# adaLN block with sliding-window attention and a token-mixing MLP: opening loads put on two DMA queues, and the last output tile cut at column 384 with a PSUM bank for each piece

## The chip, the cores and the metric

The kernel runs on one core of one Trainium2 chip. The metric is the device time of one execution in microseconds (us); smaller is better. The kernel before takes 256.79 us, the median of three runs (254.97, 256.79 and 257.36). The profile that is read here is one further execution, of 257.96 us; the span that it shows, from the core's first instruction to its last, is 256.3 us, and 1.66 us of the time lie around it.

## The reference

Everything is bf16 at the boundary. `x` has 2048 tokens of 512 columns. A condition vector `c` makes six modulation vectors, the block normalizes, attends in a window of 256 tokens with 32 heads of 16 columns, normalizes again and mixes over the tokens with an MLP of width 1792:

```python
mod = (silu(c) @ w_mod).reshape(1, 6, 1, 512)          # sa, ca, ga, sb, cb, gb
h = layernorm(x) * (1 + ca) + sa
q, k, v = split(h @ wqkv)                              # 32 heads of 16
p = softmax(where(0 <= i - j < 256, q @ k.T / 4, -1e9))
x = x + ga * ((p @ v) @ wo)
h = layernorm(layernorm(x) * (1 + cb) + sb)
u = gelu(einsum('bsd,sf->bdf', h, w1) + b1)            # over the tokens
x = x + gb * (einsum('bdf,fs->bds', u, w2) + b2).T
```

## The kernel before, in words

**Tiles.** Tokens are cut into 16 tiles of 128 (`NT`), columns into 4 slices of 128 (`ND`). `xres[t]` holds tile t of `x` in SBUF all the way through. Four groups of 512 tokens go through projection, attention (75 chunks: scores on TensorE, `et = exp` on ScalarE, a mask on VectorE, sums on TensorE), output projection and the second and third normalization. Then comes the MLP: `u` over tokens, gelu, and `y` back to tokens.

**Order.** Most of the kernel is recorded as operations with an engine each and issued in one order written out by hand (`ORDER`, run by `run_schedule`). `Ordered` wraps the engines so that the program keeps this order: on every engine, instructions run in the order in which they stand, and a waiting one holds what is behind it. Inside a helper all of these instructions carry line 256, so the profile is read by tile names. Two stretches stand outside the list: the opening loads (lines 343 to 376), issued before anything else, and the last loop (lines 1381 to 1398).

**The opening.** All loads but one go out on SyncE's DMA queue (SP): `x0`, `x1`, then the first 1024 columns of `w_mod` in four pieces of 256 KB (`wmod`, slice j = 0 to 3), then `wqkv` in pieces, then the rest. Only the 1 KB load of `c` (tile `c4`) goes out on ScalarE's queue (ACT), line 346. Each DMA has a completion semaphore; there are eight, taken in turn, so the ninth DMA issued waits, on the engine that issues it, until the first has landed, and so on.

What depends on these loads, in the order in which the engines have it:

- ScalarE: table load, (issue of `c`), `em`, `em`, `rm` (the sigmoid of `c` by exp, log, exp), the two `rs` of the first normalization, one half of the copy of the transposed tiles to `h1T`, one slice of the modulation of `h1T`.
- VectorE: statistics (`st`, `mv`) of `x0`, then `silu` (needs `rm`), then statistics of `x1`, the copy `sT`, the two normalized tiles `xn`, the other half of the copy to `h1T`, `modFM` (needs all four `wmod` slices), three slices of the modulation of `h1T`.
- TensorE: eight warm-up matmuls on a zero tile, the transpose of `silu` (`st_ps`), two more warm-ups, `fm` for slices 0 and 1 of `wmod` (tile `ps_fm`), eight transposes of `xn`, `fm` for slices 2 and 3, four warm-ups, then the first key and query projections (tiles `pss`, `pk`, `pq`), which need `h1T` and the first pieces of `wqkv`; then the first scores.

**The last loop.** For each of 16 token tiles, 14 matmuls of 512 columns add into one PSUM bank `py`; VectorE adds `xr` (a `scalar_tensor_tensor` made beforehand) and writes `otile`; SP sends it out. Banks are taken from the list `homes` in turn. The last tile is done in two halves of 256 columns, 14 matmuls each, both in the same bank, each half with its own add and its own DMA.

Of the kernel before, what the change touches and what calls it, by code (L numbers as in the profile page):

```python
# [13 lines left out]
P = 128  # L14
S = 2048
D = 512
# [3 lines left out]
NT = S // P  # L20
# [195 lines left out]
def kernel(  # L216
# [14 lines left out]
    nc = tc.nc  # L231
# [11 lines left out]
    F32 = DT.float32  # L243
# [19 lines left out]
    dma = Ordered(nc.sync)  # L263
# [63 lines left out]
    ps_od = ctx.enter_context(tc.tile_pool(name="ps_od", bufs=1, space=PSUM))  # L327
# [13 lines left out]
    c4 = modw.tile([ND, P], BF, name="c4")  # L341

    def load_x(t, queue=dma):
        queue.dma_start(out=xres[t][:], in_=x_dram[t * P : (t + 1) * P, :])

    nc.scalar.dma_start(out=c4[:], in_=c.rearrange("o (j p) -> (o j) p", p=P))

    def load_mod(j, queue):
        queue.dma_start(out=wmod[:, j, 0 : 2 * D], in_=wm_v[:, j, 0 : 2 * D])

    def load_qkv(lo, hi):
        dma.dma_start(out=wqkv[:, :, lo:hi], in_=w_v[:, :, lo:hi])

    load_x(0)
    load_x(1)
    for j in range(ND):
        load_mod(j, dma)
    load_qkv(D, D + D // 2)
    load_qkv(0, D // 2)
    load_qkv(D + D // 2, 2 * D)  # L360
# [112 lines left out]
    box = {}  # L473
# [16 lines left out]
    def e_stps(e):  # L490
# [13 lines left out]
        out=sT_rep[:], in_=sT[:].unsqueeze(2).to_broadcast([P, ND, P])), deps=[o6], pos=-6, ready=15.0)  # L504
# [64 lines left out]
    for g in range(ND):  # L569
        mod_ops.append(op("wod", "DVE", 0.34, lambda e, g=g: ve.tensor_tensor(  # L570
            out=wod[:, g, :], in0=wod[:, g, :], in1=bc_ga[:], op=ALU.mult), deps=[mod_ops[0]], pos=14.0, ready=30.0))
# [809 lines left out]
    w2r, gtmp = box["w2r"], box["gtmp"]  # L1381
    homes = ["t3", "t4", "od0", "od1", "od2", "t0", "t1", "t2"]
    for tb in range(NT):
        h = homes[tb % 8]
        py = (ps_od.tile([P, D], F32, name="py", tag=h) if h[0] == "o" else box["ps_t"].tile([P, D], F32, name="py", tag="ps" + h))
        xr = gtmp.tile([P, D], F32, name="xr")
        ve.scalar_tensor_tensor(
            out=xr[:], in0=bc_gb[:], scalar=b2FM[:, tb : tb + 1], in1=xres[tb][:], op0=ALU.mult, op1=ALU.add,
        )
        ot = gtmp.tile([P, D], BF, name="otile")  # L1390
        for cols in (slice(0, D),) if tb < NT - 1 else (slice(0, D // 2), slice(D // 2, D)):
            for n, fc in enumerate(order):
                te.matmul(
                    py[:, cols], lhsT=w2r[tb // 8][:, fc, tb % 8 * P : (tb % 8 + 1) * P], rhs=guT[fc][:, cols],
                    start=(n == 0), stop=(n == NF - 1), skip_group_check=True,
                )
            ve.tensor_tensor(out=ot[:, cols], in0=py[:, cols], in1=xr[:, cols], op=ALU.add)
            dma.dma_start(out=out_dram[tb * P : (tb + 1) * P, cols], in_=ot[:, cols])
# [31 lines left out]
```

## Time and profile before

| what | value |
|---|---|
| median of three runs | 256.79 us |
| profiled execution | 257.96 us, of which the span is 256.3 us |
| TensorE busy | 237.3 us (93% of the span) |
| VectorE busy | 209.5 us (82%) |
| ScalarE busy | 179.3 us (70%) |
| GpSimd busy | 127.6 us (50%) |
| mean granted TensorE clock | 0.993 |
| DMA | 28.12 MB, 110 GB/s over the span |
| chain that ended last | PE 52%, ACT 24%, DVE 15%, issue 5%, DMA 2%, SP's queue 1% |

The engines are PE (TensorE matmul), PEld (TensorE weight load, which overlaps PE), DVE (VectorE), ACT (ScalarE), POOL (GpSimd) and SP (SyncE); a q behind a name is the engine's own sequencer, which waits and issues DMAs. Busy shares are means over stages: in attention ScalarE runs without a break (39.79 of the 40 us from 20 to 60), in the MLP TensorE does. The chain of waits is followed back from the last instruction, at each step to what released it; its shares say which engine was being waited for. Matmuls are pipelined, so 14 matmuls of 0.38 us that start every 0.22 us are normal.

### The profile page before, as it was taken

The page shows a single profiled execution, that of the slowest core. Times are in us where ns is not written, and L with a number is a line of the kernel's source. Part 1 is how long each engine was busy: PE and PEld are TensorE (multiplying, and loading weights), DVE is VectorE, ACT ScalarE, POOL GpSimd, SP SyncE. Part 2 cuts the span into 40 slices and gives each one's busy share as a digit, 9 for nine tenths or more (in the row PEclk, how much of TensorE's full clock was granted, in tenths as well). Part 3 has the DMA queues.
Part 4 walks back from the last instruction along what each step waited for, and adds up shares of the span by engine and source line. Part 5 has one row for each costly group of instructions (what it writes and reads, how often), then busy time and mean ns, then how long its engine had stood idle before and what let it go on. Part 6 is the DMA issues. An engine that isn't in the chain of part 4 may idle for free.

```text
span 256.3 us, 9271 instructions
## 1 busy us (share of the span) xinstructions
PE 237.3 (93%) x3995; PEld 127.0 (50%) x3995; DVE 209.5 (82%) x412; ACT 179.3 (70%) x253; POOL 127.6 (50%) x225
## 2 busy tenths in 40 slices
PE   7798889899998779999999999899999999999994
PEld 3466545454554534554545455466444444444443
DVE  5579999999999999998898989999978964444442
ACT  4399999999999899999999999988136610000000
POOL 8267967799779467769773479762000000000000
PEclk9799999999999999999999999999999999999999
DMA  6998660133054200010403375322999101111111
GB/s 204 325 351 266 52 201 10 44 73 97 3 95 97 54 13 0 6 43 18 132 3 102 102 196 166 84 84 78 331 387 387 51 23 49 54 41 43 41 41 41
DMA packets 42624, 28.12 MB, mean 110 GB/s; under 512 B 12248, under 2 KB 38488, under 8 KB 42584
## 3 DMA queue, kind: packets, MB, share of 16 engines
q1 hardware_dynamic: 42576, 27.54, 36.9%
q8 instruction: 31, 0.51, 0.9%
q14 instruction: 9, 0.07, 0.1%
q10 hardware_dynamic: 8, 0.00, 0.0%
HBM read 22.03 MB, written 2.10 MB: 94 GB/s over the span
## 4 chain that ended last, share of the span: by engine, by line
PE 52%; ACT 24%; DVE 15%; issue 5%; DMA 2%; SPq 1%; DVEq 0%
ACT et L256 21%; PE py L256 19%; PE pu L256 14%; PE pss L256 6%; DVE et L256 6%; PE po L256 5%; PE pa L256 3%; ACT lz L256 2%; DVE h L256 2%; PE pk L256 2%; PE pq L256 2%; DMA wmod<-in_w_mod_dram 2%; DVE OT L256 1%; PE pv L256 1%; DVE QT L256 1%
## 5 line engine op out<-in xcount | busy, mean ns | idle before, releaser
L256 ACT ACTIVATE et<-pss 128x1536 bf16<-128x1536 f32 x75 | 110.6, 1474 | 3.6 <-PE psb L256 2.0
L256 DVE TENSOR_TENSOR et<-et,maskt 128x1024 bf16<-128x1024 bf16 (+2 forms) x79 | 49.0, 647 | 0.7 <-ACT et L256 0.7
L256 PE MATMUL py<-guT,w2r 128*128 128x512 bf16 (+1 forms) x238 | 48.7, 366 | 0.5 <-DVE otile L256 0.5
L256 ACT ACTIVATE et<-psb 128x512 bf16<-128x512 f32 x75 | 46.7, 622 | 0.0
L256 PE MATMUL pu<-hb,w1s 128*32 128x512 bf16 (+1 forms) x332 | 39.2, 380 | 0.4 <-DVE part L256 0.2
L256 PE MATMUL pss<-QT,KT 32*128 32x64 bf16 (+3 forms) x720 | 29.9, 230 | 8.7 <-ACT et L256 6.6
L256 PEld LDWEIGHTS <-w2r 128*128 128x128 bf16 x238 | 23.3, 98 | 26.0 <-issue 0.7
L256 PE MATMUL po<-et,VT 128*32 128x64 bf16 (+3 forms) x960 | 32.6, 234 | 2.2 <-DVE QT L256 0.8
L256 DVE TENSOR_TENSOR otile<-py,xr 128x512 bf16<-128x512 f32 (+1 forms) x17 | 11.2, 660 | 25.5 <-PE py L256 25.3
L256 PEld LDWEIGHTS <-KT 32*128 32x128 bf16 x960 | 16.6, 92 | 31.0 <-issue 28.6
L256 PE MATMUL po<-et,ones_bd 128*32 128x256 bf16 (+3 forms) x624 | 31.8, 268 | 0.0
L256 POOL TENSOR_SCALAR KT<-kb,mask_par 128x512 bf16<-128x512 bf16 (+1 forms) x32 | 23.2, 739 | 15.1 <-DVE kb L256 8.3
L256 PE MATMUL psb<-QT,KT 32*128 32x64 bf16 (+3 forms) x240 | 29.3, 231 | 0.0
L256 PEld LDWEIGHTS <-VT 128*32 128x32 bf16 x960 | 21.2, 96 | 15.1 <-issue 6.7
L256 DVE BATCH_NORM_STATS2 st<-x 128x6 f32<-128x512 bf16 x32 | 21.2, 679 | 1.1 <-DMA x<-in_A_x_dram 1.1
L256 PE MATMUL pk<-h1T,wqkv 128*32 128x512 bf16 (+4 forms) x216 | 21.5, 340 | 0.4 <-DVE bc_ga L256 0.3
L256 PEld LDWEIGHTS <-w1s 128*32 128x32 bf16 (+1 forms) x332 | 14.3, 97 | 15.1 <-issue 2.0
L256 PEld LDWEIGHTS <-wqkv 128*32 128x32 bf16 (+1 forms) x344 | 15.2, 98 | 11.4 <-issue 4.3
L256 PE MATMUL pa<-wod,OT 128*32 128x512 bf16 (+1 forms) x148 | 17.1, 381 | 0.9 <-DVE OT L256 0.7
L256 PE MATMUL pu<-hb,w1r 128*128 128x512 bf16 (+1 forms) x114 | 17.9, 379 | 0.0
L256 PE MATMUL pv<-wqkv,h1T 128*32 128x512 bf16 (+2 forms) x196 | 17.3, 347 | 0.1
L256 PEld LDWEIGHTS <-ones_bd 128*32 128x32 bf16 x624 | 15.9, 97 | 0.1
(111 smaller groups left out, 354.7 us busy)
## 6 DMA issues: line engine op xcount, KB each, us to landing
w2r<-in_B_w_dram SPq DMA_DIRECT2D x14, 512.0 KB, 10.5
w1s<-in_B_w_dram SPq DMA_DIRECT2D x19, 256.0 KB, 3.3
w1r<-in_B_w_dram SPq DMA_DIRECT2D x9, 256.0 KB, 4.6
x<-in_A_x_dram SPq DMA_DIRECT2D x16, 128.0 KB, 4.9
wmod<-in_w_mod_dram SPq DMA_DIRECT2D x4, 512.0 KB, 8.9
out_dram<-otile SPq DMA_DIRECT2D x15, 128.0 KB, 1.7
wmod<-in_w_mod_dram SPq DMA_DIRECT2D x4, 256.0 KB, 3.5
wqkv<-in_A_wqkv_dram SPq DMA_DIRECT2D x4, 256.0 KB, 5.6
```

The costliest lines, as they stand in the source:

```text
L256: ins = call(*args, **kwargs)
```

## The change

Two places change; the rest is the same, and apart from them each engine has the same instructions in the same order.

```diff
-    nc.scalar.dma_start(out=c4[:], in_=c.rearrange("o (j p) -> (o j) p", p=P))
...
     load_x(0)
-    load_x(1)
+    load_x(1, nc.scalar)
+    nc.scalar.dma_start(out=c4[:], in_=c.rearrange("o (j p) -> (o j) p", p=P))
     for j in range(ND):
-        load_mod(j, dma)
+        load_mod(j, nc.scalar if j % 2 else dma)
...
     for tb in range(NT):
-        h = homes[tb % 8]
-        py = (ps_od.tile([P, D], F32, name="py", tag=h) if h[0] == "o" else box["ps_t"].tile([P, D], F32, name="py", tag="ps" + h))
...
-        for cols in (slice(0, D),) if tb < NT - 1 else (slice(0, D // 2), slice(D // 2, D)):
+        for piece, cols in enumerate((slice(0, D),) if tb < NT - 1 else (slice(0, D - P), slice(D - P, D))):
+            h = homes[(tb + piece) % 8]
+            py = (ps_od.tile([P, D], F32, name="py", tag=h) if h[0] == "o" else box["ps_t"].tile([P, D], F32, name="py", tag="ps" + h))
```

SP's queue now issues `x0`, `wmod` 0, `wmod` 2 and goes on to `wqkv`; ScalarE's queue issues `x1`, `c`, `wmod` 1 and `wmod` 3 before ScalarE's first activation. The eight semaphores go, in the built program, to `x0`, `wmod` 0, `x1`, `wmod` 2, `c`, the first `wqkv` piece, `wmod` 1 and the second `wqkv` piece; `wmod` 3 is the ninth and takes over that of `x0`, so ScalarE waits there until `x0` has landed. The last tile is cut into pieces of 384 and 128 columns, the second in the next bank of `homes` (`t3`, last used by tile 8), so the second piece no longer waits for the add of the first.

## The prediction

> **What bounds the kernel now.** I read the page first. ScalarE and then TensorE are full in the middle, so only what starts that middle earlier, or shortens the end behind it, can pay. So I read the two places that change. First the chain of waits over the opening (start, length, what):
>
> ```profile
> 3.13 4.57 DMA wmod<-in_w_mod_dram
> ...
> 7.75 0.35 PE ps_fm L256 x8
> 8.10 2.16 PE pss L256 x8
> 10.26 0.43 PE pk L256 x4
> 10.68 0.85 PE pq L256 x4
> ...
> 12.47 1.45 ACT et L256
> ```
>
> The opening hangs on the fourth `wmod` slice, issued at 3.13 and landed at 7.70. Behind it come `ps_fm`, then on TensorE four warm-ups and the first key matmuls (both called `pss`), and the first `et` starts at 12.47. Next the timeline of the opening, for what stands beside that chain:
>
> ```profile
> 0.81 0.54 ACTq L346 DMA_DIRECT2D c<-in_c_dram  x1
> ...
> 2.17 0.31 ACT L256 ACTIVATE em<-c 4x128 f32<-4x128 bf16 x1
> ...
> 2.99 0.69 DVE L256 BATCH_NORM_STATS2 st<-x 128x6 f32<-128x512 bf16 x1 [1.09 <-DMA x<-in_A_x_dram]
> ...
> 3.82 0.27 DVE L256 TENSOR_TENSOR silu<-c,rm 4x128 bf16<-4x128 bf16 x1
> ...
> 6.01 0.71 PE L256 MATMUL psb<-identity,xn 128*128 128x128 bf16 x8
> ...
> 6.76 0.60 ACT L256 ACTIVATE h1T<-psb 128x512 bf16<-128x512 bf16 x1 [1.29 <-PE psb L256]
> ...
> 7.96 1.87 PE L256 MATMUL pss<-nothing 128*128 128x512 bf16 x4
> ...
> 8.40 0.60 ACT L256 ACTIVATE h1T<-h1T,modFM 128x256 bf16<-128x256 bf16 x1 [1.04 <-DVE modFM L256]
> ```
>
> A second branch runs c, `em`, `silu`, statistics of `x1`, `rs`, `xn`, transposes (6.01), copy to `h1T` (ends 7.36). It meets the first at 8.40 with 1.04 us to spare. Then the clock by stretch (start:end, length, busy us of each engine, granted clock, DMA share, GB/s):
>
> ```profile
> 4.55:7.95 3.40, 2.49 (x44) 1.74 (x44) 1.67 (x6) 1.10 (x3) 3.24 (x12) 1.00 1.02 320
> 7.96:11.36 3.40, 3.40 (x22) 1.87 (x18) 1.70 (x7) 1.23 (x3) 0.00 (x0) 0.50 1.14 321
> ```
>
> DMA is full at 320 GB/s from 4.55 on, and TensorE has half its clock from 7.96 to 11.36. Last the timeline of the end:
>
> ```profile
> 250.87 0.42 DVE L256 TENSOR_TENSOR otile<-py,xr 128x256 bf16<-128x256 f32 x1 [0.18 <-PE py L256]
> 251.35 1.69 PE L256 MATMUL py<-guT,w2r 128*128 128x256 bf16 x14 [0.51 <-DVE otile L256]
> ...
> 253.07 0.42 DVE L256 TENSOR_TENSOR otile<-py,xr 128x256 bf16<-128x256 f32 x1 [1.78 <-PE py L256]
> ```
>
> TensorE stands 0.51 us between the halves until VectorE has read the bank.
>
> **The end.** The last tile's first matmul starts at 249.14 (the timeline has the 512-wide ones every 0.216 us; the 256-wide go every 0.109: 14 of them take 1.69, the last lasting 0.27). Before: 1.53 for the first half, 0.68 until the second starts, 1.69 for it, done at 253.04. After: 384 columns lie halfway between 0.109 and 0.216, so 0.1625 each; 14 take 2.28, and the 128-wide ones start at 251.42, nothing in the way since their bank was last read at tile 8. No 128-wide `py` exists before. Its bounds are 0.109 each (the 256-wide ones: a weight load for every matmul, no gain from fewer columns) and 0.058 (the transposes of 128 columns at full clock, each with its own weight load: four take 0.40 at 16.70, the last 0.22). I take 0.058, being the same width with the same loads: 13 x 0.058 + 0.22 = 0.97, done at 252.39, 0.65 earlier; at 0.109 it would be 253.06 and nothing gained on TensorE. Weight loads do not bound it: the one-column `ps_fm` matmuls, each with its own load, go every 0.026 (eight take 0.34 at 6.56, the last 0.16).
>
> The Trainium skill (page "TensorE: Matmul & The Clock Gate", section "Back-to-back issue gap") puts a stream of weight loads and 128-wide matmuls at about 81 ns each; by that the estimate for this piece is 0.30 us longer and the forecast below 256.4. The row of 0.058 contradicts it here, so it doesn't enter the sum.
>
> The last add: 512 columns take 0.69 and 256 take 0.42, so 128 take 0.29: another 0.13. The add of 384 (0.56 by the same line) runs from 251.60 to 252.16, before the last one at 252.41; without that cover of 0.25 the last add would wait for it. SP's issue (0.33) of the first piece ends at 252.51, before the second's at 252.72. The last DMA takes 1.5 from issue to landing, as now. Sum of the end: -0.65 - 0.13 = -0.78, between -0.13 and -0.85.
>
> **The opening.** Bytes first. Ahead of and including `wmod` 3 lie 1.25 MB either way: `x0`, `x1`, four slices. With two queues that are served alike, `wmod` 3 ends when its queue's 641 KB and as many from the other have gone, and SP's queue holds `x0`, `wmod` 0 and 2, 640 KB: the same 1.28 MB. Its issue is no earlier: it waits for `x0`, which landed at 2.97, so 3.0 to 3.5 against 3.13 to 3.56. So I leave its landing at 7.7. At nothing I cost `wqkv` (same bytes ahead; `pk` and `pq` took it without waiting) and `x2`, `x3` (SP reaches them earlier; VectorE got to them at 11.90 without waiting).
>
> What is added: ScalarE issues three more DMAs before `em`, the fourth behind the wait. Each costs between 0.42 (SP's rows) and 0.54 (ACT's only row); I take 0.54. `x1` ends at 1.35, `c` at 1.94, `wmod` 1 at 2.5. `x0` now shares the engines with `x1` from the start, so it lands between 2.97 and 3.41 (when both had landed before); I take 3.3. `wmod` 3 is then issued by 3.85 and `em` starts at 3.9 instead of 2.17. Queued behind are `em`, `em`, `rm` (1.0): `silu` at 4.9 instead of 3.82. Everything behind it on VectorE moves by 1.1: `x1`'s statistics, `sT`, `xn`; then `ps_fm` 0 and 1 and the transposes, which end at 7.8, and the copy on ScalarE, from 6.76 to 7.86, ending 8.46. Of the 1.04 to spare all is used: the modulation starts at about 8.53 instead of 8.40. On TensorE `ps_fm` 2 and 3 stand behind the transposes and end at 8.25 instead of 8.10; the four warm-ups (every 0.425 at half clock) and the key matmuls move with them. Opening: +0.15. At the lower bounds (0.42, 2.97) `silu` moves by 0.78, nothing reaches the chain, and an earlier landing could give at most -0.2, since the transposes still end near 7.5. At the upper ones +0.5.
>
> **Sum.** On the profiled execution: 257.96 + 0.15 - 0.78 = 257.3. That execution stood 1.17 above the median; the same difference on 256.79 gives **256.1**, own range 255.6 to 257.2.
>
> **Rivals.**
>
> 1. *wmod 3 lands late (slower).* It goes out behind a wait while SP has four more loads up to `wqkv` 2 queued without one; if those pass first, it lands where the second `wqkv` piece landed, 4.08 + 5.4 = 9.5. It decides from about 7.9 on. Then `modFM` is 1.8 late, and so is everything to the first `et`: 257.8. If TensorE, idle till 9.5, is then not given its clock back at 11.37, the 24 `pk` matmuls (2.6 us at 0.108) and scores double: 260.4. For it: loads are full then, and this one is the last asked for. Against: on a shared queue its 2 KB packets compete with few others. Chance 0.16.
> 2. *The end pays little.* The 128-wide matmuls go every 0.109, or the output's short rows cost: 128 columns are rows of 256 bytes, half the 512 of now. A row that had to be fetched before it is written adds a read; loads of `x` took 2.2 from issue to landing and stores 1.5, so I price it 0.7. Either gives 256.8. The skill's page "DMA: Bandwidth & Descriptors", section "Specifications", says that transfers below 512 bytes are done as read-modify-write; no 256-byte store is in this trace. Chance 0.12.
> 3. *The opening gets faster.* Two queues fill the 0.57 DMA share of the first 4.5 us, `wmod` 3 lands by 7, and `silu` is not late: -0.2, so 255.8. If the warm-ups then start early enough that TensorE keeps its full clock past 7.96, the 3.4 us of half-clock work halve: 254.1. Against: `em` stands behind four issues, and in 4.55 to 7.95 TensorE would be busy less, not more, than the 2.49 that lost the clock. The change doing half of what it says belongs here: `wmod` 3 isn't shared at the start, it waits. Chance 0.10, the last part 0.03.
>
> The forecast has 0.62. Outside the range 255.0 to 257.9 lie rival 1 beyond its cheapest and the clock part of rival 3. One per cent is 2.6 us, about what a measurement can tell: the four executions shown spread over 3.0. Faster by over 1% (below 254.2) needs the clock part of rival 3 or a low set of runs: 0.05. Slower by over 1% (above 259.4) needs the dear end of rival 1: 0.07. Within: 0.88.
>
> **What would show it.** Right: no gap in PE between the last tile's pieces, 128-wide `py` every 0.058, the last add of about 0.29 near 0.8 us earlier relative to the last tile's start; `em` at 3.5 to 3.9, `silu` near 4.9, `wmod` 3 landed at 7.5 to 7.9, the first `et` at 12.3 to 12.8. Wrong: first `et` after 13.5 (rival 1) or before 12 (rival 3); a pitch near 0.1, or over 2 us from the last issue to landing (rival 2).

## The result, and the profile after

| | before | after |
|---|---|---|
| median of ten runs each, on the same chip | 256.42 us (254.58 to 257.97) | 258.40 us (257.90 to 260.27) |
| profiled execution | 257.96 us, span 256.3 | 260.27 us, span 258.6 |
| mean granted TensorE clock | 0.993 | 0.987 |
| first `et` of attention starts | 12.47 | 15.94 |
| last tile, first matmul to end of the last add | 4.35 (249.14 to 253.49) | 3.55 (252.48 to 256.03) |

The kernel became slower, by 1%: the ratio is 1.0104, with a 95% interval from 1.0066 to 1.0143. Here and in the experiments the ratio and its interval are worked out from the executions that were not slow (over 1.5% above the fastest of their kernel), while the medians are over all of them, so the two don't follow from each other (without the slow ones, kernels 12 and 14 below stand at -0.88 and -1.16). The forecast was 256.1, with a range of 255.0 to 257.9. The profiled execution of after is the slowest of its ten, 1.87 above their median, so its opening shows the loss larger than it usually is.

The chain of waits of the kernel after, over the opening (start, length, what):

```profile
3.48 7.64 DMA wmod<-in_w_mod_dram
...
11.17 0.37 PE ps_fm L256 x8
11.55 0.24 issue
11.79 1.91 PE pss L256 x7
13.70 0.43 PE pk L256 x4
14.13 0.87 PE pq L256 x4
...
15.94 1.45 ACT et L256
```

It is the same chain as before, link by link, and from `ps_fm` to `et` it takes 4.77 where it took 4.72. What grew is its first link: slice 3 of `wmod`, issued at 3.48 instead of 3.13, takes 7.64 us to land instead of 4.57, until 11.13. The timeline of the opening of the kernel after shows what stands around it:

```profile
1.85 1.97 ACTq L347 DMA_DIRECT2D wmod<-in_w_mod_dram  x2
...
2.19 3.52 SPq L256 DMA_DIRECT2D wqkv<-in_A_wqkv_dram  x4
...
3.86 0.31 ACT L256 ACTIVATE em<-c 4x128 f32<-4x128 bf16 x1 [1.80 <-DMA c<-in_c_dram]
...
4.88 0.28 DVE L256 TENSOR_TENSOR silu<-c,rm 4x128 bf16<-4x128 bf16 x1 [0.49 <-ACT rm L256]
...
8.89 0.37 PE L256 MATMUL ps_fm<-sT,wmod 128*128 128x1 bf16 x8 [2.47 <-DMA wmod<-in_w_mod_dram]
9.12 1.01 PE L256 MATMUL psb<-identity,xn 128*128 128x128 bf16 x8
...
11.17 0.37 PE L256 MATMUL ps_fm<-sT,wmod 128*128 128x1 bf16 x8 [0.85 <-DMA wmod<-in_w_mod_dram]
```

ScalarE's queue issues two slices between 1.85 and 3.82, the second only when `x0` has landed (3.46). In that time SP's queue has gone on to `wqkv` from 2.19. And slice 1 is late too: TensorE waits 2.47 us for it until 8.89, with the eight transposes queued behind.

Each DMA adds to its completion semaphore once for each of the 16 DMA engines, and the trace has the time of every addition. For the kernel after (worked out from the trace, us):

```
                      issued, on    8th engine   15th    last
slice 2               1.72  SP         6.01      6.81    8.63
slice 1               1.85  ACT        6.25      7.02    8.84
wqkv, first piece     2.19  SP         6.93      7.67    9.52
wqkv, second piece    2.66  SP         7.76      8.55   10.68
slice 3               3.48  ACT        8.49      9.34   11.13
wqkv, third piece     4.17  SP         9.39     10.12   11.87
before: slice 3       3.13  SP         6.71      6.92    7.70
```

Two things are seen. Down the columns, the pieces land in the order in which they were issued, whichever queue they are on: slice 1 is 0.24 us behind slice 2, and each later one 0.7 to 0.9 behind the one above it; slice 3 comes two places of `wqkv` later than it did. Along the rows, one engine is 1.7 to 2.1 us behind the other fifteen, and a slice counts only when that one has brought its part. A single packet of 2 KB that started at 4.61 took 1.57 us, where the median of that size took 0.08; the trace does not say on which engine it was.

The clock by stretch of the kernel after, columns as before:

```profile
4.88:8.28 3.40, 1.05 (x11) 0.55 (x11) 1.84 (x6) 0.50 (x2) 3.06 (x12) 1.00 1.03 327
8.29:11.69 3.40, 1.81 (x32) 1.70 (x34) 0.53 (x3) 0.60 (x1) 0.00 (x0) 0.50 0.95 247
11.70:15.10 3.40, 3.19 (x15) 1.86 (x15) 1.67 (x8) 1.23 (x3) 0.00 (x0) 0.50 1.02 344
```

TensorE, waiting for slices, is busy 1.05 of 3.40 us and then 1.81; its clock is halved for two stretches instead of one.

The end, in the timeline of the kernel after:

```profile
251.83 3.87 PE L256 MATMUL py<-guT,w2r 128*128 128x512 bf16 x31
...
254.96 0.56 DVE L256 TENSOR_TENSOR otile<-py,xr 128x384 bf16<-128x384 f32 x1 [0.92 <-PE py L256]
255.74 0.29 DVE L256 TENSOR_TENSOR otile<-py,xr 128x128 bf16<-128x128 f32 x1 [0.22 <-PE py L256]
```

The matmuls of both pieces are one unbroken group with those of the tile before (31 of them, no gap on TensorE). The last tile takes 0.80 us less.

### The profile page after: what moved, and what is told of

Read it like the earlier page. It is cut to its first block, busy times and chain, and to the rows that moved or that the text cites. A ratio compares the mean times of both kernels' runs of the same rounds, so it can differ in the third digit from the quotient of the medians.

```text
span 258.6 us, 9246 instructions
## 1 busy us (share of the span) xinstructions
PE 235.2 (91%) x3970; PEld 127.0 (49%) x3995; DVE 209.4 (81%) x412; ACT 179.3 (69%) x253; POOL 127.1 (49%) x225
## 4 chain that ended last, share of the span: by engine, by line
PE 53%; ACT 24%; DVE 14%; DMA 4%; issue 4%; DVEq 0%
ACT et L256 21%; PE py L256 19%; PE pu L256 14%; PE pss L256 6%; PE po L256 6%; DVE et L256 5%; PE pa L256 3%; DMA wmod<-in_w_mod_dram 3%; ACT lz L256 2%; DVE h L256 2%; PE pq L256 2%; PE pk L256 2%; DVE OT L256 1%; PE pv L256 1%; DVE QT L256 1%
## 5 line engine op out<-in xcount | busy, mean ns | idle before, releaser
L256 PE MATMUL py<-guT,w2r 128*128 128x512 bf16 (+2 forms) x234 | 48.3, 366 | 0.2
L256 PE MATMUL pu<-hb,w1s 128*32 128x512 bf16 (+1 forms) x324 | 38.5, 380 | 1.0 <-DVE part L256 0.4
L256 DVE TENSOR_TENSOR otile<-py,xr 128x512 bf16<-128x512 f32 (+2 forms) x17 | 11.2, 660 | 24.5 <-PE py L256 22.7
```

Of the source, the lines that this page charges most:

```text
L256: ins = call(*args, **kwargs)
```

## The experiments

"Difference" is the kernel's median less the median of before on the same chip; the interval belongs to the ratio to it. The first `et` comes from one profiled execution each.

| kernel | difference, us | ratio and 95% interval | GB/s from 4 to 5 us | last slice landed | first `et` |
|---|---|---|---|---|---|
| before (its profile) | | | 320 | 7.70 | 12.47 |
| the change | +1.98 | 1.0104 (1.0066 to 1.0143) | 196 | 11.13 | 15.94 |
| 1 opening alone | +3.65 | 1.0130 (1.0074 to 1.0187) | 203 | 10.01 | 14.48 |
| 2 end alone | -1.13 | 0.9950 (0.9909 to 0.9990) | 297 | 6.91 | 10.71 |
| 3 one queue, slice 3 late | +2.87 | 1.0110 (1.0041 to 1.0178) | 287 | 9.02 | 13.47 |
| 4 two queues, slice 3 early | +2.15 | 1.0103 (1.0066 to 1.0139) | 381 | 7.50 | 13.29 |
| 5 c, x1 on ACT, slices on SP | +0.40 | 1.0026 (0.9988 to 1.0064) | 410 | 6.92 | 11.86 |
| 6 x1, c on ACT, slices on SP | +0.26 | 1.0012 (0.9978 to 1.0047) | 254 | 7.85 | 12.29 |
| 7 end alone, fill matmuls | -0.43 | 0.9979 (0.9947 to 1.0011) | 383 | 7.16 | 11.13 |
| 8 change, fill matmuls | +2.78 | 1.0106 (1.0032 to 1.0179) | 283 | 9.51 | 13.41 |
| 9 end alone again | -0.78 | 0.9967 (0.9937 to 0.9997) | 326 | 7.47 | 11.04 |
| 10 change, slice 3 on SP | +2.37 | 1.0109 (1.0081 to 1.0137) | 233 | 8.85 | 14.66 |
| 11 change, slice 1 on SP | +2.02 | 1.0077 (1.0038 to 1.0116) | 217 | 8.82 | 14.25 |
| 12 end alone, slice 1 on ACT | -0.58 | 0.9967 (0.9934 to 1.0001) | 375 | 7.25 | 10.85 |
| 13 as 10, c ahead of x1 | +0.18 | 1.0009 (0.9981 to 1.0037) | 392 | 6.88 | 11.02 |
| 14 as 12, slices 1, 3 on ACT | -0.55 | 0.9955 (0.9914 to 0.9997) | 305 | 8.01 | 12.85 |
| 15 change, c ahead of x1 | +2.46 | 1.0089 (1.0061 to 1.0117) | 405 | 8.52 | 13.52 |
| 16 as 10, c on SP | -0.06 | 1.0002 (0.9968 to 1.0036) | 373 | 6.81 | 11.19 |

Kernels 1, 3 and 4 have the old end; the others have the new one. Most kernels had 9 to 12 runs; 1, 3 and 8 had four and 10 had six.

### Each half alone (1, 2, 9)

1 is the changed opening with the old last loop, 2 and 9 the old opening with the new last loop.

> Theory 'order': the loads are served in the order in which they are issued, whichever queue they are on; slice 3 of wmod was issued at 3.48, behind two wqkv pieces (2.19 and 2.66), and so landed late. Theory 'queue': what goes out on the second queue is served late or slowly whenever it is issued. Both expect the whole loss of the change here, in the opening alone: slice 3 landed at 10 to 11.5, the first et at 15 to 16 (12.47 before, 15.94 after), the time 2.3 to 3.3 us above the kernel before. If the end were part of the loss, this kernel would stand less than 2 us above.

> The end alone, opening as before. Both theories: 128-wide py every 0.056 us, no gap between the pieces, 0.8 us less from the last tile's first matmul to the end of its last add (4.35 before, 3.55 after); the time 0.5 to 1.0 us below the kernel before. Anything slower than the kernel before would put part of the loss into the end.

> The same kernel as the end alone (old opening, last tile in pieces of 384 and 128 columns), once more on another chip. Theory: the end is worth 0.8 us in every execution, so the ratio to the kernel before is 0.997 (0.8 of 256), and the lower ratio of the first measurement (0.995) held some luck with TensorE's clock. Rival: the end alone changes nothing that lasts, ratio 1.000. Last tile from first matmul to last add 3.55 us either way.

The loss is the opening's: +3.65 alone, more than the 2.3 to 3.3 that was expected, with the first `et` at 14.48, earlier than expected. The end alone gains 1.13 and 0.78 on two chips, and its last tile takes 3.55 us (245.84 to 249.39), as in the change. So it is faster than both kernels of this case, and none of the others is clearly faster than it (7, 12 and 14 lie within the intervals). Nothing in it touches the opening, and yet its first `et` starts at 10.71 and 11.04 where the profile of before has 12.47: both of these have the full clock from 6.1 us on. So the profile of before shows one of its slower openings.

### The order of issue (3, 4)

3 keeps all loads on SP's queue and only moves slice 3 behind two pieces of `wqkv`; 4 has the changed opening with `c` first and on SP's queue, so that slice 3 is no longer the ninth DMA:

```diff
 # 3, from before
-    for j in range(ND):
+    for j in range(ND - 1):
         load_mod(j, dma)
     load_qkv(D, D + D // 2)
     load_qkv(0, D // 2)
+    load_mod(ND - 1, dma)
 # 4, the changed opening
+    dma.dma_start(out=c4[:], in_=c.rearrange("o (j p) -> (o j) p", p=P))
     load_x(0)
     load_x(1, nc.scalar)
-    nc.scalar.dma_start(out=c4[:], in_=c.rearrange("o (j p) -> (o j) p", p=P))
```

> One queue as before, but slice 3 of wmod is issued behind two wqkv pieces; no second queue, no later em. Theory 'order': this alone brings most of the loss: slice 3 landed at 9 to 10, the first et at 14 to 15, the time 1.5 to 2.5 us above the kernel before. If the loss is in the second queue itself (two queues that disturb each other, a late em), slice 3 still lands two pieces later (1.8 us), but the opening keeps at least 1.5 us of the 3.4 us that the change lost.

> Two queues as in the change (x1 and slices 1 and 3 on ScalarE's), but c is issued first on SyncE's queue, so slice 3 needs no wait and is issued at about 1.8, before any wqkv piece. Old end. Theory 'order': slice 3 lands at 7 to 8, the first et at 12 to 13, the time within 1 us of the kernel before. Theory 'queue': slice 3 lands after 9.5 all the same, the first et after 14, the time over 1.5 us above.

The timeline of kernel 3, where no second queue is used:

```profile
4.16 0.50 SPq L256 DMA_DIRECT2D wmod<-in_w_mod_dram  x1
...
9.07 0.35 PE L256 MATMUL ps_fm<-sT,wmod 128*128 128x1 bf16 x8 [2.06 <-DMA wmod<-in_w_mod_dram]
...
13.47 1.45 ACT L256 ACTIVATE et<-pss 128x1536 bf16<-128x1536 f32 x1 [1.16 <-PE pss L256]
```

Slice 3 is issued a microsecond later and lands 1.3 later than before, and the first `et` with it: the loss of 2.87 comes from order alone (four runs; 1.5 to 2.5 was expected). In kernel 4 slice 3 goes out on ScalarE's queue at 1.72 and lands at 6.96, ahead of slice 2 (issued 2.11, landed 7.50): that queue is not slow as such. But kernel 4 loses 2.15 all the same, which the order theory did not have. `x0` is issued second there, and `silu` comes at 4.79 instead of 3.82. Its profile, set beside that of 9 with the old opening, has the loss in two parts: `modFM` comes at 8.72 beside 7.90, since slice 0 (issued 1.65) has its last engine only at 6.76, 1.58 behind its eighth, and holds `ps_fm` until 6.81; and from `modFM` to the first `et` it takes 4.57 beside 3.14, since TensorE works at half pace until 13.43. Why slice 0's last engine is late and why the clock is lost there was not tested.

### Slices back on SP (5, 6)

```diff
 # 6, from after
-        load_mod(j, nc.scalar if j % 2 else dma)
+        load_mod(j, dma)
 # 5, the same and c ahead of x1
+    nc.scalar.dma_start(out=c4[:], in_=c.rearrange("o (j p) -> (o j) p", p=P))
     load_x(0)
     load_x(1, nc.scalar)
-    nc.scalar.dma_start(out=c4[:], in_=c.rearrange("o (j p) -> (o j) p", p=P))
```

> Only c and then x1 on ScalarE's queue, all four slices of wmod on SyncE's, new end. Theory 'order': slice 3 is issued at about 2.7, before any wqkv piece, lands at 6.5 to 7.2, em at 2.2 and silu below 4.3; the first et at 10.3 to 12.5 depending on TensorE's clock, the time as the end alone (0.3 below to 0.5 above it). Theory 'two queues disturb each other': slice 3 lands after 7.7 and the time is over 1 us above the end alone.

> As the kernel before this one in the list, but x1 in front of c on ScalarE's queue, as the change has it: the late c branch without the late slice. The prediction's sum: silu at 4.5 to 4.9, the transposes end at 7.5 to 7.8, the spare time takes it; the time within 0.5 us of the kernel with c first. If the branch has no spare time once slice 3 is early, the first et comes 0.5 to 1.2 us later than there at the same clock.

With the slices on one queue the loss is gone to +0.40 and +0.26. In 6 `em` starts as late as in the change (3.88) and `silu` at 4.90; in 5 they are at 2.21 and 3.81. There is no clear difference between the two, so the late `em` is hidden. Both still lack the end's gain: they are 1.0 to 1.5 above the end alone (2 and 9), as the second theory expected of the time, though slice 3 came as early in 5 (6.92) as the first expected.

### Keeping the clock (7, 8)

Matmuls whose results are not used are put ahead of `ps_fm` of slice 3 (7, with the old opening) and of slices 1 and 3 (8, with the changed one), in the same scratch bank as the warm-ups (the counts of 8 are `{1: 8, 3: 4}`):

```diff
+            for i in range({3: 4}.get(k, 0)):
+                te.matmul(box["warm"][:, i % 3, :], lhsT=warm[:, 0:P], rhs=warm[:], start=True, stop=True)
```

> Opening as before, new end, and four more warm-up matmuls on TensorE (their result is not used) in its wait for slice 3. Theory 'clock': TensorE keeps its full clock past the opening in more executions, the granted clock is 0.998 or more in nearly all, the median 0.3 to 1.0 us below that of the end alone, the first et below 11 in the profile. If the clock is worth nothing, the median equals that of the end alone or is up to 0.5 us above it (the added matmuls in the way of ps_fm).

> The change, with eight more warm-up matmuls in the wait for slice 1 and four in the wait for slice 3. The late slice stays: landed after 9.5. Theory 'order, with the clock on top': the clock is held while TensorE waits, from the landing of slice 3 to the first et it is 3.6 to 4.0 us instead of 4.8, and the time is 0.8 to 1.8 us below the change (258.4), still over 1 us above the end alone. If the late slice costs through the clock alone, the time comes down to that of the end alone.

In the two profiles the clock was held: full from 4.43 us on in 7 and from 4.82 on in 8. What it is worth there is seen on the first key projections (`pk`). In kernel 9, at full clock, they start every 0.055 us:

```profile
9.26 0.39 PE L256 MATMUL pk<-h1T,wqkv 128*128 128x128 bf16 x4
```

In kernel 15 (below), at half clock, they start every 0.107:

```profile
10.89 0.63 PE L256 MATMUL pk<-h1T,wqkv 128*128 128x128 bf16 x4
```

From `modFM` to the first `et` it takes 3.13 us in 7 and in 8 and 3.14 in 9, and 4.0 to 4.6 in 1, 3, 4, 10, 11 and 15, whose TensorE works at half pace for most of that time. So in these profiles the lost clock adds 0.9 to 1.4. But 8, with the full clock, has `modFM` at 10.28 where 9 has 7.90, and loses 2.78 (four runs, a wide interval; 0.8 to 1.8 below the change was expected): the late slices lose enough by themselves, and the lost clock comes on top. The added matmuls also stand in the way: slice 3 landed at 9.51 in 8, and its `ps_fm` started at 9.90. 7 is no faster than the end alone, whose two profiles have the full clock without them.

The mean granted clock of an execution doesn't tell whether its opening had the full clock. It takes what lies ahead of the first record of the clock for full, and in 4, 11 and 15 that record is at 13.43, 13.89 and 13.33: all three show a mean of 1.000 over an opening at half pace. So the ten runs of 7, all at 1.000, don't show for each that the clock was held, and two of the four runs of 8 (0.993 and 0.992) lost some of it.

### Slice 3 early again, and the second cost (10, 11)

```diff
 # 10, from after
-        load_mod(j, nc.scalar if j % 2 else dma)
+        load_mod(j, nc.scalar if j == 1 else dma)
 # 11: j == 3
```

> The change with slice 3 of wmod alone put back on SP's queue; x1, c and slice 1 stay on ScalarE's queue, em is as late as in the change. Order theory (what was issued first lands first, whichever queue): slice 3 is issued near 2.2 us without a wait, ahead of all wqkv pieces, lands between 7.0 and 7.9, the first et starts between 11.8 and 12.8, and the median is within 0.6 us of the kernel before (256.3 beside 256.0). Rival (two loaded queues as such are the loss, each gets half of the engines): slice 3 lands near 7.7 but slice 1 on ScalarE's queue lands past 9, the first et comes after 14, and the median is 1.5 to 2 us above the kernel before.

> The change with slice 1 alone put back on SP's queue; slice 3 stays on ScalarE's queue. With one DMA fewer ahead of it, slice 3 is the seventh DMA in the program and takes no semaphore over, so it is issued near 1.9 us without a wait. Order theory: it lands between 6.5 and 7.9, before or with slice 2, the first et starts between 11.8 and 12.8, and the median is within 0.6 us of the kernel before. Rival (ScalarE's queue is served late as such): slice 3 lands past 9 again, the first et after 14, and the median is 1.5 to 2 us above the kernel before.

The order theory was right about the order and wrong about the time. In both kernels all slices are issued by 2.18, ahead of every piece of `wqkv`, and the eighth engine has the last one at 6.46 and 6.66, no later than that of slice 3 in the kernel before (6.71). But the last engine has it only at 8.85 and 8.82, and 2.37 and 2.02 us are lost. The rivals had the loss and the late first `et` about right, but not for their reasons: in 10 slice 1 lands at 8.36, not past 9, and in 11 slice 3 on ScalarE's queue lands at 8.32, with slice 2 of SP's at 8.82 behind it, so neither queue is preferred. A second cost was there that the order theory did not have.

### What brings the second cost (12, 13, 14, 16)

```diff
 # 12, from 2:
-        load_mod(j, dma)
+        load_mod(j, nc.scalar if j == 1 else dma)
 # 14, from 2:
+        load_mod(j, nc.scalar if j % 2 else dma)
 # 13, from 10 (15: the same from after):
+    nc.scalar.dma_start(out=c4[:], in_=c.rearrange("o (j p) -> (o j) p", p=P))
     load_x(1, nc.scalar)
-    nc.scalar.dma_start(out=c4[:], in_=c.rearrange("o (j p) -> (o j) p", p=P))
 # 16, from 10:
-    nc.scalar.dma_start(out=c4[:], in_=c.rearrange("o (j p) -> (o j) p", p=P))
+    dma.dma_start(out=c4[:], in_=c.rearrange("o (j p) -> (o j) p", p=P))
```

> The end alone (old opening, new last loop) with one thing more: slice 1 of wmod goes out on ScalarE's queue, behind c and near 1.35 us; x0, x1, slices 0, 2 and 3 stay on SP's queue, nothing waits for a semaphore, and em starts on time (below 2.5). Theory (as soon as slices come over both queues at once, some of the 16 DMA engines fall behind the others, and a slice counts only when the last engine has brought its part): the last engine of the last three slices comes 1.0 to 2.1 us behind the eighth, the last slice lands between 8.0 and 9.0 though it was issued before every wqkv piece, the first et starts between 13 and 14.7, and the median is 0.8 to 2 us above the kernel before. Rival (the loss with slice 1 on ScalarE's queue needs the late em and x1's load on that queue): all slices land by 7.7, the first et starts between 10.7 and 12.6, and the median is 0.3 to 0.9 below the kernel before, like the end alone.

> The change with slice 3 of wmod on SP's queue, as in the kernel that lost 2.4 us, and with c ahead of x1 on ScalarE's queue: c, x1, slice 1. So c lands by 2.2 and em starts on time (below 2.5), and x0 and x1 no longer start in the same moment; slice 1 still goes out on ScalarE's queue beside slice 2 on SP's. Theory A (the loss comes with two loads of wmod that run beside each other, behind x1 on the other queue): DMA moves less than 260 GB/s between 4 and 5 us, the last engine of slices 1 and 2 comes 1.3 us or more behind the eighth, transposes wait for ps_fm of slice 1, first et after 13.8, median 1.5 to 2.5 above the kernel before. Theory B (it comes with x0 and x1 starting together, or with c behind x1): over 300 GB/s between 4 and 5, slices by 7.5, first et between 10.7 and 12.6, median 0.9 below to 0.4 above the kernel before.

> The end alone with slices 1 and 3 of wmod on ScalarE's queue behind c; x0, x1, slices 0 and 2 on SP's queue. Order of issue: x0, c, x1, slice 1 (near 1.4), slice 0 (1.7), slice 3 (1.9), slice 2 (2.2), then wqkv. Theory A (two loads of wmod beside each other lose): slices 2 and 3 show last engines 1.3 us or more behind the eighth, the last lands past 8, first et after 13, median 0.8 to 2 above the kernel before. Theory B (only the start of x0 with x1, or c behind x1, loses): slices land by 7.5, first et between 10.7 and 12.6, median 0.3 to 0.9 below the kernel before, like the end alone; em may start up to 0.4 later for the second issue.

> The kernel that lost 2.4 us (the change with slice 3 on SP's queue), with c moved to SP's queue behind x0. So x0 and x1 still start in the same moment on two queues, but c no longer stands behind x1, and slices 0, 2, 3 are issued one place later. If the loss comes with x0 and x1 starting together: below 290 GB/s between 4 and 5 us, slices 1 and 2 past 7.7 on their last engine, first et after 13.2, median 1.2 to 2.5 above the kernel before. If it comes with c behind x1 on ScalarE's queue: over 300 GB/s, slices by 7.6, first et below 12.6, median 0.9 below to 0.6 above. em starts near 2.7 to 3.9 in both.

12 and 14 refute that slices on two queues lose by themselves: -0.58 and -0.55, as good as the end alone within their intervals. (The profiled execution of 14 is one of its slowest, with half clock until 16.31 and slices at 8.01; its median tells the verdict, not that profile.) 13 differs from 10 in nothing but the order of `c` and `x1` on ScalarE's queue, and goes from +2.37 to +0.18. 16 leaves `x0` and `x1` starting together and takes `c` to SP's queue: -0.06. So the loss comes with `c` behind `x1` on ScalarE's queue, not with the joint start.

The timeline of kernel 10:

```profile
3.45 0.31 ACT L256 ACTIVATE em<-c 4x128 f32<-4x128 bf16 x1 [1.38 <-DMA c<-in_c_dram]
...
8.40 0.37 PE L256 MATMUL ps_fm<-sT,wmod 128*128 128x1 bf16 x8 [2.40 <-DMA wmod<-in_w_mod_dram]
8.64 1.01 PE L256 MATMUL psb<-identity,xn 128*128 128x128 bf16 x8
```

The same of kernel 13:

```profile
2.27 0.31 ACT L256 ACTIVATE em<-c 4x128 f32<-4x128 bf16 x1 [0.20 <-DMA c<-in_c_dram]
...
6.37 0.35 PE L256 MATMUL ps_fm<-sT,wmod 128*128 128x1 bf16 x8 [0.25 <-DMA wmod<-in_w_mod_dram]
...
11.02 1.45 ACT L256 ACTIVATE et<-pss 128x1536 bf16<-128x1536 f32 x1 [0.73 <-PE pss L256]
```

In 10 it isn't `em` that holds TensorE (`xn` was ready long before) but slice 1, at 8.40 where 13 has 6.37. The stretch from 4 to 5 us by engine, clock and DMA in kernel 10 (the last two columns are DMA share and GB/s):

```profile
4.00:5.00 1.00, 0.86 (x5) 0.19 (x3) 0.77 (x4) 0.40 (x2) 1.00 (x1) 1.00 0.91 233
```

In kernel 13:

```profile
4.00:5.00 1.00, 1.00 (x5) 0.19 (x3) 0.30 (x2) 0.00 (x0) 1.00 (x1) 1.00 1.10 392
```

And in kernel 16:

```profile
4.00:5.00 1.00, 0.87 (x3) 0.00 (x0) 0.64 (x4) 0.65 (x3) 1.00 (x1) 1.00 1.04 373
```

DMA slackens to 233 GB/s in 10 and does not in 13 and 16; in 10 two packets of 2 KB that start at 5.2 take 1.37 and 1.34 us, and slice 1 lands 2.36 us after its eighth engine (6.00 to 8.36), in 13 0.57 (5.76 to 6.33). In three pairs that differ in the order of these two loads alone, DMA moves 196 and 405 GB/s from 4 to 5 us (the change and 15), 233 and 392 (10 and 13), 254 and 410 (6 and 5), one profile each. All six kernels with `c` behind `x1` on ScalarE's queue (the change, 1, 6, 8, 10, 11) have the lowest rates of the table, 196 to 283, though the next is at 287 (3). Kernel 6 has the slack too (254) and loses little; no slice of its goes out beside one on the other queue, but that this is why was not tested. Why `c`, four packets of 256 bytes, does this was not found: no kernel here looks into a DMA engine.

### The late place alone, on two queues (15)

15 is the whole change with only these two loads swapped, so that the second cost is out and slice 3 is still the ninth DMA:

> The whole change, with c ahead of x1 on ScalarE's queue and nothing else different: em starts later than 2.5 only because slice 3's issue, still the ninth DMA, waits for x0 first (near 3.0). Order theory (the late place of slice 3 in the order of issue loses by itself, whatever the start does): slice 3 is issued between 2.9 and 3.4 behind two wqkv pieces of SP's, lands between 8.4 and 9.8, the first et starts between 12.6 and 14.5, and the median is 0.8 to 2 us above the kernel before. Rival (with c ahead of x1 all four slices come in time, the late place costs little since ScalarE's queue has nothing else then): slice 3 by 7.9, first et below 12.5, median within 0.6 of the kernel before.

The timeline of kernel 15:

```profile
1.78 1.47 ACTq L347 DMA_DIRECT2D wmod<-in_w_mod_dram  x2
...
2.18 3.26 SPq L256 DMA_DIRECT2D wqkv<-in_A_wqkv_dram  x4
...
8.57 0.38 PE L256 MATMUL ps_fm<-sT,wmod 128*128 128x1 bf16 x8 [0.60 <-DMA wmod<-in_w_mod_dram]
...
13.52 1.45 ACT L256 ACTIVATE et<-pss 128x1536 bf16<-128x1536 f32 x1 [1.34 <-PE pss L256]
```

Slice 3 is issued at 2.91, behind two pieces of `wqkv`, and lands at 8.52, its last engine 0.3 behind the eighth (8.21); DMA moves 405 GB/s from 4 to 5. The kernel loses 2.46, more than the 0.8 to 2 expected. Its first `et` is 2.48 later than that of 9: 1.08 of it stands ahead of `modFM` (8.98 beside 7.90), where slice 3 decides, and 1.40 behind it, where TensorE works at half pace. So the change has two separate costs, each of some 2 us beside before: the late place of slice 3 (3 and 15) and `c` behind `x1` beside a slice on the same queue (10 and 11). They don't add: the first holds up `ps_fm` of slice 3 (8.57 in 15), the second `ps_fm` of slice 1 with the transposes behind it (8.40 in 10), links of the same chain on TensorE. Taking away either one alone gives nothing back (+2.46 and +2.37 beside +1.98 of the change); with both away, in 13, the loss is gone (+0.18).

## Why the prediction was wrong

**The step that failed** is in the opening: "With two queues that are served alike, `wmod` 3 ends when its queue's 641 KB and as many from the other have gone ... So I leave its landing at 7.7". The queues were not served by turns from the moment of issue; pieces landed in the order of issue over both queues. So what counts ahead of slice 3 is everything issued before 3.48, and SP had by then put out two pieces of `wqkv`, 0.52 MB. At the 320 GB/s of the profile before that is 0.52 / 0.32 = 1.6 us. The eighth engine, which had slice 3 at 6.71 before, would then have it at 8.3, and had it at 8.49; the last, 7.70 before, would have it at 9.3, and had it at 11.13, with 1.8 us between the fifteenth engine and the last that order does not explain. The step saw both facts that it needed (the wait for `x0`, and SP's loads without one) and set them in the rival instead.

The Trainium skill (page "DMA: Bandwidth & Descriptors", section "Queues, rings and completion order") says that each engine goes round between the queues it has work for, one packet at a time. That is the sharing which the step took. The trace agrees only for loads in flight together (kernel 15: the second piece of `wqkv`, issued 2.66, and slice 3, issued 2.91 on the other queue, have their eighth engines at 8.32 and 8.21); slice 3 of the change, issued 0.8 and 1.3 us behind two pieces of the other queue, didn't get past them.

**Rival 1 is one half of what happened**, by its mechanism and near its price: "if those pass first, it lands where the second `wqkv` piece landed, 4.08 + 5.4 = 9.5", giving 257.8, and 260.4 if the clock is lost too. Measured: 11.13 in the slowest run, 10.01 and 9.51 in two other looks at this opening, a median of 258.4, and a profiled run of 260.27 with the half clock until 15.11. It had 0.16, because its 2 KB packets would "compete with few others" on their queue; but ScalarE's queue starts no packet between 6.4 and 7.0, while `wqkv`'s packets of 512 bytes had moved since 4.9. Kernel 15, which has this half alone, has slice 3 at 8.52, a microsecond ahead of the rival's 9.5, and loses as much, with 1.40 us of it behind `modFM` at half pace.

**Not in the prediction at all:** slice 1 late. It was taken for landed in time, so that the transposes hang on `xn`; it landed at 8.84 and held them until 9.12, and the copy to `h1T`, expected to end at 8.46, ended at 10.77. Nor the slackening of DMA with `c` behind `x1`, the other half: no row of the profile before shows it.

**The base.** The sum was made on an execution with a half-clock opening (first `et` at 12.47), where the same opening at full clock gives 10.71 and 11.04. With those as base, the first `et` less 10.71, less 0.8 where the new end is in, gives the measured difference within 1 us for all kernels but the change and 14, whose profiled runs were among their slowest: 15, for one, 13.52 - 10.71 - 0.8 = +2.0 beside +2.46.

**Right:** the start of the second branch (`em` predicted 3.9, measured 3.86; `silu` 4.9, 4.88; slice 3 issued by 3.85, measured 3.48), and that a late `em` alone costs next to nothing (5 beside 6). But the time of `em` was partly luck. It was put down to ScalarE's issues, and in kernel 6, where ScalarE issues no slice, it is as late:

```profile
3.88 0.31 ACT L256 ACTIVATE em<-c 4x128 f32<-4x128 bf16 x1 [1.82 <-DMA c<-in_c_dram]
```

There `c`, behind `x1` on its queue, lands only at 3.86 (2.14 in before). The prediction had no such term; in the change `c` landed at 3.55, and the issue of slice 3, which ended at 3.82, came last.

The end was right in its terms too, -0.78 predicted and -0.80 measured: 128-wide `py` every 0.0555 (0.058 taken), 384-wide every 0.1625, as predicted, adds of 0.56 and 0.29, the gap gone.

**Rival 2 fell.** The pitch is below its 0.109, and also below the 81 ns that the Trainium skill's page "TensorE: Matmul & The Clock Gate", section "Back-to-back issue gap", gives for a stream of weight loads and 128-wide matmuls: here 14 in a row, each with its weight load, kept 55.5. The last DMA, rows of 256 bytes, took 1.47 us from issue to landing (256.06 to 257.53) beside 1.53 for the rows of 512 (and twice the bytes) before, so no read was added that could be seen.

**Rival 3 fell:** the second queue filled the early DMA share (3 to 4 us: 303 GB/s beside 246) and lost it from 4 to 5 (196 beside 320). The end's gain is real and is given back three to five times over in the opening (3.65 lost in 1, 0.78 to 1.13 gained in 9 and 2).

**Still open:** what stalls a DMA engine or a packet for over 1 us when `c` stands behind `x1`; why kernel 4 loses its clock and has slice 0 late; why TensorE loses its clock in some of these openings and not in others; and why the kernels that keep `x1` on ScalarE's queue without either cost (5, 6, 13, 16) stand at -0.06 to +0.40, while those with `x1` on SP's (2, 7, 9, 12, 14) stand at -0.43 to -1.13, though 13 and 16 start their first `et` as early (11.02 and 11.19) as 7 and 9 (11.13 and 11.04).

## What to carry to other kernels

When loads move to a second queue, write out the issue times of both queues as one list: what the chain waits for must stand early in that list, and a load that has to wait for a semaphore before it can be issued falls behind everything that the other queue issues meanwhile. Count the DMAs up to the number of completion semaphores, and keep the one that the chain hangs on within it. And profile an opening more than once before costing a change on it: here one and the same opening differed by 1.8 us between executions.

## What the hardware showed that was not expected

- Completion of a DMA is set by its slowest engine: slice 2 of the change had fifteen engines by 6.81 and the last at 8.63. Single 2 KB packets took up to 1.57 us, where the median is 0.08; one of 0.96 is in the profile before too.
- The order of two loads on a queue, one of them 1 KB, went with DMA rates of 233 and 392 GB/s in a later microsecond (10 and 13), and with 196 and 405, and 254 and 410, in two more pairs.
- The clock is granted in stretches of 3.413 us that begin at another place in each execution (4.54, 4.87, 5.08, 6.26 in four profiles), and whether an opening runs at half clock changes with the execution: the old opening had half the clock from 7.96 to 11.37 in the profile of before and the full clock in those of 2 and 9. The Trainium skill, page "TensorE: Matmul & The Clock Gate", section "What's actually happening", says that this window runs freely and doesn't begin with the kernel; the traces agree.
- A mean granted clock of 1.000 can stand over an opening at half clock (4, 11 and 15), so the pace of the matmuls is what to look at.
